# RWKV-5 scores by one product with 128 keys in place of two with 64, on one core

## The chip, the core and the metric

The kernel runs on one core of a Trainium2 chip. The metric is device time in microseconds of one execution. Three executions of the kernel before took 389.34, 387.3 and 390.62 us, median 389.34. The engines are named as in the profile: PE (TensorE; PEld are its weight loads), DVE (VectorE), ACT (ScalarE), POOL (GpSimd), SP (SyncE, which issues the loads). All data is fp32.

## What is computed

Two blocks, one after the other. The first is a linear recurrence over 768 tokens with 4 batches and 8 heads of 48 channels, the second a mixture of experts on its output:

```python
# attention: r, k, v are (4, 8, 768, 48); w, u are (8, 48)
for t in range(S):
    cur = einsum('bhd,bhe->bhde', u[None] * kt, vt)
    y[:, :, t] = einsum('bhd,bhde->bhe', rt, state + cur)
    state = w[None, :, :, None] * state + einsum('bhd,bhe->bhde', kt, vt)

# experts: x = y as (4, 768, 384), E = 8, F = 1024
e = argmax(logits[b, s]) if s == 0 or local_gate[b, s] < 0.5 else prev_e
out[b, s] = softmax(logits[b, s])[e] * (relu(x[b, s] @ w1[e]) @ w2[e])
```

## The kernel before

**Attention.** The work is cut into 16 items: 4 batches by 4 pairs of heads. The two heads of a pair lie on partitions 0 to 47 and 64 to 111. Time is cut into 6 chunks (NCH) of 128 tokens (P). Inside a chunk, the recurrence becomes a matrix of scores between 128 keys and 128 queries, masked so that a query sees only earlier keys; between chunks a state of 48 by 48 per head is carried. For each item n (functions of class `Attention`):

- `load` (L194): SP loads r and k turned (tile rk), k and v by token (kv) and v turned (vT), three items ahead.
- `scale` (L208): POOL makes ke (k times powers of w counted from the chunk's end, L217, from the table endT), rw (r times powers of w, L234; for the first three items DVE does it, in halves) and pd (r times k, L221).
- `keys` (L236): DVE makes kw, k over powers of w (L241).
- `added` (L245): PE multiplies ke by v, the sum that each chunk adds to the state (L253). `states` (L255): DVE scans these sums over the chunks into S (L259).
- `scores` (L275), called twice, for chunks 0 to 2 and 3 to 5: PE multiplies kw by rw (L288) into one of two PSUM pairs of banks, one bank per head, and DVE masks the result into tile am (L290).
- `own` (L262): PE sums u times pd over channels (L269) into tile y in PSUM, and DVE multiplies it by vT (L273).
- `inside` (L292): PE adds v times am to y (L297). `before` (L301): PE adds S times rw to y (L310), and ACT copies y to xT (L314), after which y is free for the next item's `own`.
- `turn` (L317): PE transposes xT (L323) and ACT copies it to x (L325), which goes to memory once per batch (L328). At the end of a batch, `logits` (L336) and `token_logits` (L342) make the router's inputs.

There is one y, there are two pairs of banks (shared by scores, transposes and logits, taken in turn by `banks`), two am, three rw. The order on every engine is written out by hand in `run` (L345): for an item n from 3 on it is turn(n-2), keys(n), added(n), states(n), scale(n+1), inside(n-1), before(n-1), scores(n) twice with the first mask, own(n), the second mask. From item 9 on, routing for the first two batches is put between these steps (on DVE mostly; items 13 and 14 have a step of it between the first mask and the product L273).

**The scores before.** A product of fp32 is two records of load and product in the profile. For each chunk and head, the 128 keys are taken as two halves of 64, each a product of its own (`o`). The half of later keys needs only the later 64 queries (`x`), except in the first item, where the tiles in PSUM are written in full. In odd chunks the halves change places in the 128 partitions of the result (`f`), and v (and k, in the same tile kv) is stored in that order by the host (`_tokens`). So four products lie on four quarters of the array: rows by head, columns by key half.

```python
for o in range(2):
    for h in range(2):
        q, f = slice(h * DP, h * DP + DH), c % 2 ^ o
        x = o * DP if n else 0
        nc.tensor.matmul(sc[f * DP:(f + 1) * DP, h, i, x:], lhsT=t["kw"][q, c, o * DP:(o + 1) * DP],
                         rhs=t["rw"][q, c, x:], start=True, stop=True)
```

The swap needs a second mask and a second table of end powers: `kept` (made on POOL at L1591 to L1595, doubled on ACT at L1596), and `end`, `endT` in two orders (`ends` L167 and L168, `turn_ends` L174 and L175).

**Experts.** From about 119 us on, PE multiplies blocks of tokens, gathered by expert, by w1 and w2 (L1064, L1114, L1151, L1183); POOL gathers and scatters rows. The change doesn't touch this part. `general_attention` (L477) runs only for values of w outside a range that the inputs don't have.

Of the kernel before, what the change touches and what calls it, by code (L numbers as in the profile page):

```python
# [11 lines left out]
F32 = mybir.dt.float32  # L12
# [8 lines left out]
P = 128  # L21
B, H, S, DH = 4, 8, 768, 48
HP = H // 2
# [32 lines left out]
def spread(ap, axis, n):  # L56

    a = ap.unsqueeze(axis)
    return a.to_broadcast([n if i == axis else s for i, s in enumerate(a.shape)])


class Attention:
# [10 lines left out]

    def __init__(self, tc, st, rk_d, kv_d, vT_d, x_d, w_t, wp_d, kept, ident, lt, mp):
        self.tc, self.nc = tc, tc.nc
        nc = tc.nc
        self.rk_d, self.kv_d, self.vT_d, self.x_d = rk_d, kv_d, vT_d, x_d
        self.w_t, self.kept, self.ident, self.lt = w_t, kept, ident, lt  # L80

        self.late = st.enter_context(tc.tile_pool(name="late", bufs=1))
        self.wp = self.late.tile([P, H, 32], F32, name="wp")
        self.sel = self.late.tile([P, 2 * (E + 1)], F32, name="sel")
        self.inner = ExitStack()

        def pool(name, bufs, **kw):
            return self.inner.enter_context(tc.tile_pool(name=name, bufs=bufs, **kw))

        once = pool("once", 1)  # L90
        self.two = pool("two", 2)
        self.three = pool("three", 3)
# [36 lines left out]
        n = 2  # L129
        while n <= P:  # L130
            m = min(n - 1, P + 1 - n)
            for engine, t in ((nc.vector, tab[:, :1]), (nc.gpsimd, tab[:, 1:])):
                engine.tensor_mul(t[..., n:n + m], t[..., 1:1 + m], t[..., n - 1:n].to_broadcast([P, t.shape[1], 2, m]))
            n += m

        self.first, self.newton = mp[:, :P + 1], mp[:, P + 1:2 * P + 1]
        nc.scalar.copy(self.first, tab[:, 0, 0])
        self.reciprocals(0)

        self.end = once.tile([P, HP, P + DP], F32, name="end")  # L140
        self.endT = once.tile([P, 2, HP, 2 * DH], F32, name="endT")
        self.align(26)
        self.warm(8)
        self.ends(slice(0, 1))
        self.turn_ends(slice(0, 1))
        self.warm(5)
# [17 lines left out]
            self.nc.tensor.transpose(t[:, i % 2, :P], self.ident, self.ident)  # L164

    def ends(self, z):
        self.nc.scalar.copy(self.end[:, z, :P], self.tab[:, z, 0, P - 1::-1])  # L167
        self.nc.scalar.copy(self.end[:, z, P:], self.tab[:, z, 0, P - 1:DP - 1:-1])  # L168

    def turn_ends(self, z):  # L170
        ep, n = self.banks("ep"), z.stop - z.start
        for k in range(n):
            for o in range(2):
                self.nc.tensor.transpose(ep[:, o, k * P:(k + 1) * P], self.end[:, z.start + k, o * DP:o * DP + P], self.ident)  # L174
        self.nc.scalar.copy(self.endT[:, :, z].rearrange("p o i (h d) -> p o (i h) d", h=2),  # L175
                            ep[:, :, :n * P].rearrange("p o (i d) -> p o i d", d=DP)[..., :DH])

    def tables(self):

# [28 lines left out]
    def scale(self, n):  # L208

        nc, t = self.nc, self.items[n]  # L210
        t["ke"] = self.two.tile([P, NCH, 2 * DH], F32, name="ke")
        t["pd"] = self.two.tile([P, NCH, P], F32, name="pd")
        t["rw"] = self.three.tile([P, NCH, P], F32, name="rw")
        hp = t["hp"]

        def ke(p):
            nc.gpsimd.tensor_mul(t["ke"][:, p::2], t["k"][:, p::2], spread(self.endT[:, p, hp], 1, C2))  # L217

        def pd(i):
            z = slice(i * C2, (i + 1) * C2)  # L220
            nc.gpsimd.tensor_mul(t["pd"][:, z], t["rT"][:, z], t["kT"][:, z])  # L221

        def rw(i):
            self.decayed(nc.gpsimd, n, slice(i * C2, (i + 1) * C2))


        for what in (ke, rw, pd) if n > 2 else (pd, ke):
            for i in range(2):
                what(i)
# [45 lines left out]
    def scores(self, n, g):  # L275

        nc, t = self.nc, self.items[n]
        if g == 0:
            t["am"] = self.two.tile([P, 2, 2, 3, P], F32, name="am")
        sc = self.banks("sc")[:, :, :3 * P].rearrange("p h (c t) -> p h c t", t=P)  # L280
        for i in range(3):
            c = 3 * g + i
            for o in range(2):
                for h in range(2):
                    q, f = slice(h * DP, h * DP + DH), c % 2 ^ o

                    x = o * DP if n else 0
                    nc.tensor.matmul(sc[f * DP:(f + 1) * DP, h, i, x:], lhsT=t["kw"][q, c, o * DP:(o + 1) * DP],  # L288
                                     rhs=t["rw"][q, c, x:], start=True, stop=True)
        return lambda: nc.vector.tensor_mul(t["am"][:, g], sc, spread(self.kept[:, g:g + 3], 1, 2))  # L290

    def inside(self, n):  # L292
        nc, t = self.nc, self.items[n]
# [183 lines left out]
def general_attention(tc, rk_d, kv_d, wu, wg_d, x_d, ident, lt):  # L477

    nc = tc.nc
    with tc.tile_pool(name="g1", bufs=1) as g1, tc.tile_pool(name="g2", bufs=2) as g2, \  # L480
# [3 lines left out]
        nc.vector.memset(ones, 0.0)  # L484
        for i in range(2):
            nc.vector.memset(ones[i * DP:(i + 1) * DP, i:i + 1], 1.0)
        turned = g1.tile([P, P], F32, name="g_turned")
        nc.vector.tensor_copy(turned[:, :DP], ident[:, DP:])
        nc.vector.tensor_copy(turned[:, DP:], ident[:, :DP])
        with tc.For_i(0, HP, 1) as hp:  # L490
            wu_t = g1.tile([P, 2], F32, name="g_wu")
            nc.sync.dma_start(out=wu_t, in_=wu[bass.ds(hp, 1)].rearrange("o p x -> (o p) x"))
            with tc.For_i(0, B, 1) as b:
# [11 lines left out]
                for e in range(DH):  # L505
                    vp = gps.tile([P, 2, 512], F32, name="g_vp")
                    for c in range(NCH):
                        for i in range(2):
                            nc.tensor.matmul(
                                vp[i * DP:(i + 1) * DP, c // 3, (c % 3) * P:(c % 3 + 1) * P],  # L510
                                lhsT=v_t[:, c, i, e:e + 1].to_broadcast([P, DP]),
                                rhs=turned if c % 2 else ident,
                                start=True, stop=True)
                    kv = g2.tile([P, S], F32, name="g_kv")
                    nc.vector.tensor_mul(kv.rearrange("p (g t) -> p g t", g=2),
# [1046 lines left out]
def kernel(  # L1562
# [23 lines left out]
    nc.gpsimd.affine_select(out=mask, in_=mask, compare_op=Alu.is_ge, fill=0.0, base=-1,  # L1586
                            channel_multiplier=-1, pattern=[[1, P]])

    kept = keep.tile([P, 4, P], F32, name="kept")
    lo, hi = slice(0, DP), slice(DP, P)  # L1590
    nc.gpsimd.tensor_copy(kept[:, 0], mask)  # L1591
    nc.gpsimd.memset(kept[lo, 1, lo], 0.0)
    nc.gpsimd.tensor_copy(kept[lo, 1, hi], mask[lo, lo])
    nc.gpsimd.tensor_copy(kept[hi, 1, lo], mask[hi, hi])
    nc.gpsimd.memset(kept[hi, 1, hi], 1.0)  # L1595
    nc.scalar.copy(kept[:, 2:], kept[:, :2])  # L1596
    lt = keep.tile([P, NC, E + 1], F32, name="lt")

    gid = keep.tile([P, E * ST], I32, name="gid")
# [4 lines left out]
    with ExitStack() as st, tc.manual_schedule():  # L1604
# [1 line left out]
        mpp = st.enter_context(tc.tile_pool(name="mpp", bufs=1, space=PSUM))  # L1606
        router = Router(tc, ro, mpp, lt, mask, ident, gid, sid, gate, over[:, 0:1])
        ex = Experts(tc, st, x_d, w1, w2, out, ident, router)
        att = Attention(tc, st, rk_d, kv_d, vT_d, x_d, w_t, wp_d, kept, ident, lt, router.mp)
        att.run(router, lambda: ex.fetch(0, nc.sync), lambda: ex.gather(0))  # L1610
        ex.open(st)
        router.open(1, st.enter_context(tc.tile_pool(name="ro1", bufs=1)))
# [49 lines left out]

def _tokens(a, np):

    x = a.reshape(B, HP, 2, NCH, 2, DP, DH)
    x = np.stack([x[:, :, :, c, ::-1 if c % 2 else 1] for c in range(NCH)], 2)
    return x.transpose(0, 1, 4, 5, 2, 3, 6).reshape(B, HP, P, NCH * 2 * DH)


# [35 lines left out]
```

## Time and profile before

| what | us |
|---|---|
| median of three runs | 389.34 |
| profiled execution, its own time | 388.15 |
| its span in the profile | 386.4 |
| attention: first score product to last product L310 | 7.4 to 115.8 |
| first expert product L1064 | 119.5 |
| L288, scores on PE, busy | 22.4 |
| L290, masking on DVE, busy | 30.1 |
| L269, busy | 14.1 |
| L297, busy | 28.9 |

A line of the profile gives the program's line, the engine, the operation, its tiles as out<-in, shapes as partitions by elements, and a count. In timelines the columns are start and length in us of a run of like instructions, and in brackets the engine's idle time before it with what ended it. "issue" there is idle time in which no semaphore was awaited. Matmul records overlap: their lengths include the passage through the array, so the time from first start to last end is what counts.

### The profile page before, as it was taken

How to read it: one execution, taken by the hardware profiler on the slowest of the kernel's cores; microseconds unless marked ns; L12 is line 12 of the kernel's file. 1: busy time of each engine (PE TensorE's matmuls, PEld its weight loads, DVE VectorE, ACT ScalarE, POOL GpSimd, SP SyncE). 2: the span in 40 equal slices, each digit the busy share in tenths (PEclk: the TensorE clock that was granted, in tenths of full speed). 3: DMA queues.
4: the chain of work that ended last, by engine and by line, in shares of the span. 5: the costliest groups of instructions: out<-in, count | busy, mean ns of one | idle time of the engine just before them, and what ended most of it. 6: DMA issues, size and time to landing. Idle time of an engine off the chain costs nothing. (4 is left out here: it accounts for less than half of the span.)

```text
span 386.4 us, 9723 instructions
## 1 busy us (share of the span) xinstructions
PE 371.5 (96%) x3858; PEld 328.5 (85%) x3858; DVE 247.1 (64%) x718; ACT 107.6 (28%) x293; POOL 151.1 (39%) x212
## 2 busy tenths in 40 slices
PE   7999999799999999999999999999999999999992
PEld 6776877677777999998999999999999999999971
DVE  7887576588954564587657757758757758556400
ACT  4132232222213111322323233234224234222220
POOL 8769998696322022611333222312403213012022
PEclk9999999999999999999999999999999999999998
DMA  7999998979213982740552145245156146064011
GB/s 257 414 409 410 409 405 274 355 256 394 99 32 101 378 338 64 249 185 23 184 179 108 42 170 213 66 171 204 56 185 224 38 165 227 21 199 181 2 37 37
DMA packets 17477, 74.97 MB, mean 194 GB/s; under 512 B 2729, under 2 KB 6586, under 8 KB 14864
## 3 DMA queue, kind: packets, MB, share of 16 engines
q1 hardware_dynamic: 10048, 56.89, 39.1%
q0 software_dynamic: 3424, 9.52, 7.4%
q10 hardware_dynamic: 3952, 7.87, 5.6%
q8 instruction: 32, 0.52, 0.6%
q14 instruction: 21, 0.17, 0.1%
HBM read 64.83 MB, written 9.51 MB: 192 GB/s over the span
## 5 line engine op out<-in xcount | busy, mean ns | idle before, releaser
L1263 POOL DMA_INDIRECT out_dram<-yo,sid x27 | 26.6, 986 | 102.3 <-ACT yo L1258 78.8
L1114 PE MATMUL h<-exT,w1t 128*128 128x168 f32 (+4 forms) x240 | 54.9, 327 | 0.0
L1118 DVE TENSOR_TENSOR hT<-h,hs 128x168 f32<-128x168 f32 (+3 forms) x60 | 21.1, 351 | 46.5 <-PE h L1114 30.4
L1037 POOL DMA_INDIRECT xg<-x_d,gid x29 | 31.1, 1073 | 38.2 <-DVE sm L872 17.4
L1114 PEld LDWEIGHTS h<-exT,w1t 128*128 128x128 f32 x240 | 41.7, 190 | 0.3 <-issue 0.3
L290 DVE TENSOR_TENSOR am<-pair,kept 128x768 f32<-128x768 f32 x32 | 30.1, 952 | 16.8 <-PE pair L288 16.4
L1064 PE MATMUL h<-exT,w1t 128*128 128x192 f32 (+1 forms) x192 | 38.2, 337 | 0.0
L1183 PE MATMUL y<-factors,sums 128*128 128x192 f32 x168 | 36.8, 326 | 0.0
L1114 PE MATMUL h<-xs,ws 128*128 128x168 f32 (+4 forms) x144 | 35.2, 326 | 0.0
L1064 PEld LDWEIGHTS h<-exT,w1t 128*128 128x128 f32 x192 | 32.3, 190 | 1.4 <-issue 0.2
L221 POOL TENSOR_TENSOR pd<-rk 128x384 f32<-128x384 f32 x32 | 31.9, 1017 | 3.0 <-DMA rk<-in_rk_dram 2.2
L297 PE MATMUL y<-am,kv 128*64 128x128 f32 x384 | 28.9, 278 | 3.4 <-issue 2.2
L1114 PEld LDWEIGHTS h<-xs,ws 128*128 128x128 f32 x144 | 25.5, 190 | 4.3 <-ACT hs L1121 1.2
L1183 PEld LDWEIGHTS y<-factors,sums 128*128 128x128 f32 x168 | 28.9, 190 | 0.0
L297 PEld LDWEIGHTS y<-am,kv 128*64 128x64 f32 x384 | 24.8, 136 | 4.7 <-issue 2.4
L234 POOL TENSOR_TENSOR rw<-rk,tab 128x384 f32<-128x384 f32 x26 | 23.6, 931 | 7.3 <-PE y L310 7.3
L217 POOL TENSOR_TENSOR ke<-kv,endT 128x288 f32<-128x288 f32 x32 | 24.9, 799 | 3.9 <-DMA kv<-in_kv_dram 3.0
L314 ACT COPY xT<-y 128x768 f32<-128x768 f32 (+1 forms) x16 | 12.5, 779 | 42.3 <-PE y L310 42.3
L288 PE MATMUL pair<-rw,kw 48*64 48x128 f32 (+1 forms) x768 | 22.4, 249 | 1.3 <-ACT end L168 0.6
L1183 PE MATMUL y<-w2t,hT 128*128 128x192 f32 x96 | 23.0, 328 | 0.0
L1051 DVE COPY exT<-tp 128x384 f32<-128x384 f32 (+6 forms) x29 | 14.0, 489 | 12.8 <-PE tp L1050 12.6
L288 PEld LDWEIGHTS pair<-rw,kw 48*64 48x64 f32 x768 | 19.4, 133 | 2.7 <-issue 0.9
(279 smaller groups left out, 733.0 us busy)
## 6 DMA issues: line engine op xcount, KB each, us to landing
w1t<-in_w_dram SPq DMA_DIRECT2D x9, 1536.0 KB, 6.7
w2t<-in_w_dram SPq DMA_DIRECT2D x9, 1536.0 KB, 7.3
rk<-in_rk_dram SPq DMA_DIRECT2D x15, 768.0 KB, 9.4
kv<-in_kv_dram SPq DMA_DIRECT2D x16, 584.0 KB, 9.1
vT<-in_vT_dram SPq DMA_DIRECT2D x16, 384.0 KB, 7.4
x_d<-x ACTq DMA_DIRECT2D x4, 1152.0 KB, 10.7
w1t<-in_w_dram ACTq DMA_DIRECT2D x1, 1536.0 KB, 10.2
w2t<-in_w_dram ACTq DMA_DIRECT2D x1, 1536.0 KB, 13.5
```

What stands on the lines that cost most here:

```text
L217: nc.gpsimd.tensor_mul(t["ke"][:, p::2], t["k"][:, p::2], spread(self.endT[:, p, hp], 1, C2))
L221: nc.gpsimd.tensor_mul(t["pd"][:, z], t["rT"][:, z], t["kT"][:, z])
L234: engine.tensor_mul(t["rw"][:, z], t["rT"][:, z], spread(pw, 1, z.stop - z.start))
L288: nc.tensor.matmul(sc[f * DP:(f + 1) * DP, h, i, x:], lhsT=t["kw"][q, c, o * DP:(o + 1) * DP], rhs=t["rw"][q, c, x:], start=True, stop=True)
L290: return lambda: nc.vector.tensor_mul(t["am"][:, g], sc, spread(self.kept[:, g:g + 3], 1, 2))
L297: nc.tensor.matmul(t["y"][p * DP:(p + 1) * DP, h, c2 * P:(c2 + 1) * P], lhsT=t["v"][:, (2 * c + h) * DH:(2 * c + h) * DH + DP], rhs=t["am" ...
L1037: self.nc.gpsimd.indirect_dma_start(out=xg[:n], out_offset=None, in_=self.x_d[:rows], in_offset=bass.IndirectOffsetOnAxis(ap=u["gid"][:n, ...
L1064: nc.tensor.matmul(h[:, :n], lhsT=u["w1"][:, m, kk, :], rhs=u["xT"][:, kk, :], start=(kk == 0), stop=(kk == DK - 1))
L1114: nc.tensor.matmul(out, lhsT=a, rhs=b, start=start and k == 0, stop=stop and k == len(terms) - 1, skip_group_check=True)
L1118: nc.vector.tensor_tensor(out, a, b, op=Alu.add)
L1183: return lambda: nc.tensor.matmul(bank[:, x * half:(x + 1) * half], lhsT=a, rhs=b, start=(j == 0 and x == 0), stop=(j == FK // 2 - 1), ski ...
L1263: self.nc.gpsimd.indirect_dma_start(out=out.rearrange("n (h d) -> (n h) d", h=2) if half else out, out_offset=bass.IndirectOffsetOnAxis(ap ...
```

## The change

For each chunk and head there is one product: 128 keys, 128 queries, with the result on all 128 partitions. Keys are in the same order in every chunk, so one mask serves all chunks, read three times over by DVE, and one table of end powers. ke is made for chunks 0 to 2 and then 3 to 5, in place of even and then odd ones. The host stores k and v in plain order.

```diff
-        self.end = once.tile([P, HP, P + DP], F32, name="end")
-        self.endT = once.tile([P, 2, HP, 2 * DH], F32, name="endT")
+        self.end = once.tile([P, HP, P], F32, name="end")
+        self.endT = once.tile([P, HP, 2 * DH], F32, name="endT")
...
     def ends(self, z):
-        self.nc.scalar.copy(self.end[:, z, :P], self.tab[:, z, 0, P - 1::-1])
-        self.nc.scalar.copy(self.end[:, z, P:], self.tab[:, z, 0, P - 1:DP - 1:-1])
+        self.nc.scalar.copy(self.end[:, z], self.tab[:, z, 0, P - 1::-1])
...
         for k in range(n):
-            for o in range(2):
-                self.nc.tensor.transpose(ep[:, o, k * P:(k + 1) * P], self.end[:, z.start + k, o * DP:o * DP + P], self.ident)
+            self.nc.tensor.transpose(ep[:, 0, k * P:(k + 1) * P], self.end[:, z.start + k], self.ident)
...
-        def ke(p):
-            nc.gpsimd.tensor_mul(t["ke"][:, p::2], t["k"][:, p::2], spread(self.endT[:, p, hp], 1, C2))
+        def ke(i):
+            z = slice(i * C2, (i + 1) * C2)
+            nc.gpsimd.tensor_mul(t["ke"][:, z], t["k"][:, z], spread(self.endT[:, hp], 1, C2))
...
             c = 3 * g + i
-            for o in range(2):
-                for h in range(2):
-                    q, f = slice(h * DP, h * DP + DH), c % 2 ^ o
-
-                    x = o * DP if n else 0
-                    nc.tensor.matmul(sc[f * DP:(f + 1) * DP, h, i, x:], lhsT=t["kw"][q, c, o * DP:(o + 1) * DP],
-                                     rhs=t["rw"][q, c, x:], start=True, stop=True)
-        return lambda: nc.vector.tensor_mul(t["am"][:, g], sc, spread(self.kept[:, g:g + 3], 1, 2))
+            for h in range(2):
+                q = slice(h * DP, h * DP + DH)
+                nc.tensor.matmul(sc[:, h, i], lhsT=t["kw"][q, c], rhs=t["rw"][q, c], start=True, stop=True)
+        return lambda: nc.vector.tensor_mul(t["am"][:, g], sc, spread(spread(self.mask, 1, 3), 1, 2))
...
-    kept = keep.tile([P, 4, P], F32, name="kept")
-    lo, hi = slice(0, DP), slice(DP, P)
-    nc.gpsimd.tensor_copy(kept[:, 0], mask)
-    nc.gpsimd.memset(kept[lo, 1, lo], 0.0)
-    nc.gpsimd.tensor_copy(kept[lo, 1, hi], mask[lo, lo])
-    nc.gpsimd.tensor_copy(kept[hi, 1, lo], mask[hi, hi])
-    nc.gpsimd.memset(kept[hi, 1, hi], 1.0)
-    nc.scalar.copy(kept[:, 2:], kept[:, :2])
...
-    x = a.reshape(B, HP, 2, NCH, 2, DP, DH)
-    x = np.stack([x[:, :, :, c, ::-1 if c % 2 else 1] for c in range(NCH)], 2)
-    return x.transpose(0, 1, 4, 5, 2, 3, 6).reshape(B, HP, P, NCH * 2 * DH)
+    return a.reshape(B, HP, 2, NCH, P, DH).transpose(0, 1, 4, 3, 2, 5).reshape(B, HP, P, NCH * 2 * DH)
```

`general_attention` loses the turned identity that undid the swap.

More of the change, by code (lines that the diff above doesn't have):

```diff
@@ L62, with __init__ @@
 class Attention:
-    def __init__(self, tc, st, rk_d, kv_d, vT_d, x_d, w_t, wp_d, kept, ident, lt, mp):
+    def __init__(self, tc, st, rk_d, kv_d, vT_d, x_d, w_t, wp_d, mask, ident, lt, mp):
         self.tc, self.nc = tc, tc.nc
@@ L79, in __init__ @@
         self.rk_d, self.kv_d, self.vT_d, self.x_d = rk_d, kv_d, vT_d, x_d
-        self.w_t, self.kept, self.ident, self.lt = w_t, kept, ident, lt
+        self.w_t, self.mask, self.ident, self.lt = w_t, mask, ident, lt
         self.late = st.enter_context(tc.tile_pool(name="late", bufs=1))
@@ L172, in turn_ends @@
         for k in range(n):
-            for o in range(2):
-                self.nc.tensor.transpose(ep[:, o, k * P:(k + 1) * P], self.end[:, z.start + k, o * DP:o * DP + P], self.ident)
-        self.nc.scalar.copy(self.endT[:, :, z].rearrange("p o i (h d) -> p o (i h) d", h=2),
-                            ep[:, :, :n * P].rearrange("p o (i d) -> p o i d", d=DP)[..., :DH])
+            self.nc.tensor.transpose(ep[:, 0, k * P:(k + 1) * P], self.end[:, z.start + k], self.ident)
+        self.nc.scalar.copy(self.endT[:, z].rearrange("p i (h d) -> p (i h) d", h=2),
+                            ep[:, 0, :n * P].rearrange("p (i d) -> p i d", d=DP)[..., :DH])
     def tables(self):
@@ L486, in general_attention @@
             nc.vector.memset(ones[i * DP:(i + 1) * DP, i:i + 1], 1.0)
-        turned = g1.tile([P, P], F32, name="g_turned")
-        nc.vector.tensor_copy(turned[:, :DP], ident[:, DP:])
-        nc.vector.tensor_copy(turned[:, DP:], ident[:, :DP])
         with tc.For_i(0, HP, 1) as hp:
@@ L511, in general_attention @@
                                 lhsT=v_t[:, c, i, e:e + 1].to_broadcast([P, DP]),
-                                rhs=turned if c % 2 else ident,
+                                rhs=ident,
                                 start=True, stop=True)
@@ L1608 @@
         ex = Experts(tc, st, x_d, w1, w2, out, ident, router)
-        att = Attention(tc, st, rk_d, kv_d, vT_d, x_d, w_t, wp_d, kept, ident, lt, router.mp)
+        att = Attention(tc, st, rk_d, kv_d, vT_d, x_d, w_t, wp_d, mask, ident, lt, router.mp)
         att.run(router, lambda: ex.fetch(0, nc.sync), lambda: ex.gather(0))
```

## The prediction

> **What bounds the kernel now.** I read the page first, then busy time by stage, then the sum of waits, then the timeline of single items. A change of 1% (3.9 us) is about what a measurement of this kernel can tell from no change. The page:
>
> ```profile
> span 386.4 us, 9723 instructions
> PE 371.5 (96%) x3858; PEld 328.5 (85%) x3858; DVE 247.1 (64%) x718; ACT 107.6 (28%) x293; POOL 151.1 (39%) x212
> ...
> POOL out_dram L1263 0%
> ...
> L288 PE MATMUL pair<-rw,kw 48*64 48x128 f32 (+1 forms) x768 | 22.4, 249 | 1.3 <-ACT end L168 0.6
> ```
>
> The chain that ended last is of no use here: it stops at the final scatter (0% of the span). PE is busy 96%, but the scores (L288) hold only 22.4 us of it, all in attention. So the stage decides:
>
> ```profile
> core 0: us, PE busy (x) PEld busy (x) DVE busy (x) ACT busy (x) POOL busy (x), PEclk, DMA share, GB/s
> 10.00:60.00 50.00, 47.97 (x1006) 37.88 (x1007) 37.40 (x73) 12.79 (x32) 44.80 (x61) 1.00 1.01 404
> 60.00:119.00 59.00, 55.73 (x1095) 41.51 (x1088) 42.48 (x74) 15.00 (x33) 34.15 (x38) 1.00 0.62 221
> ```
>
> From 10 to 60 us the DMA share is full and POOL is at 44.80 of 50, which looks like two other bounds. The waits say no: in all of attention POOL waited for rk and kv only 5.2 us, in the first four items, and its longest recurring wait (L234, 7.3 us) is for a buffer that PE frees. Loads and POOL run ahead and are held back by PE. What sets an item's period is read in one undisturbed item (number 7):
>
> ```profile
> 52.14 0.49 PE L297 MATMUL y<-am,kv 128*64 128x128 f32 x3
> ...
> 52.56 1.30 PE L310 MATMUL y<-rw,S 48*48 48x128 f32 x20
> ...
> 53.68 1.19 PE L288 MATMUL pair<-rw,kw 48*64 48x128 f32 x48
> 53.92 0.80 ACT L314 COPY xT<-y 128x768 f32<-128x768 f32 x1 [2.91 <-PE y L310]
> 54.48 0.96 DVE L290 TENSOR_TENSOR am<-pair,kept 128x768 f32<-128x768 f32 x1 [1.57 <-PE pair L288]
> ...
> 54.87 0.88 PE L269 MATMUL y<-pd,w_t 48*64 48x384 f32 x8
> 55.67 0.58 PEld L323 LDWEIGHTS pair<-ident,xT 112*128 112x128 f32 x6 [0.60 <-DVE am L290]
> ...
> 55.86 0.97 DVE L273 TENSOR_TENSOR y<-y,vT 128x768 f32<-128x768 f32 x1 [0.42 <-PE y L269]
> ...
> 56.88 1.94 PE L297 MATMUL y<-am,kv 128*64 128x128 f32 x24
> ```
>
> A ring: the state product L310 ends at 53.86; ACT copies y out (ends 54.72) while PE does the scores (53.68 to 54.87); then L269 may overwrite y (54.87), DVE multiplies it (55.86 to 56.83), L297 starts at 56.88, then L310 of the next item. So L269 starts 1.01 us after L310's end, gated by the copy, with the scores ending just as it starts. The scores have almost no cover to grow into. Two more rows price the change:
>
> ```profile
> 11.50 1.55 PE L297 MATMUL y<-am,kv 128*64 128x128 f32 x24
> ```
>
> ```profile
> PEld y L310 <- issue: 3.1, 16, 0.4
> ...
> PEld y L297 <- issue: 2.4, 1, 2.4
> ```
>
> **The change part by part.**
>
> *Scores.* Per chunk and head, before: two products of 64 keys, one with 128 and (from item 1 on) one with 64 moving columns; a product is two records. An item has 48 records, on four quarters of the array (head by key half), and takes 1.19 us from first start to last end. After: 24 records, all with 128 moving columns, on two halves (head only, each 48 rows by 128 columns). The nearest row is L297 at 11.50: also 24 records of 128 moving columns on two halves of the array, nothing awaited: 1.55 us. So fewer instructions take 0.36 us longer: the masked quarter that was skipped is now computed, and in each of the two halves 12 records follow each other at about 0.11 us.
>
> *Two changes of shape.* Before, L310, L288 and L269 all ran on quarters, and L288 started 0.18 us ahead of L310's end (53.68 against 53.86). Where the shape changes, from L297 to L310, the next product started only 0.07 us ahead of the end (52.56 against 52.63); that is the 0.17 to 0.19 us of idle per item in the wait of L310 for "issue" (3.1 over 16). After, this change comes twice more, before and after the scores. New ring: scores start 0.07 before L310's end, last 1.55, L269 starts 0.07 before their end: 1.55 - 0.14 = 1.41 us after L310's end against 1.01 now. Delay per item +0.40 us. L269 to L323 (0.08 ahead) and L323 to L253 (0.06) agree. Low end, no price for the change of shape: 1.55 - 0.36 = 1.19, +0.18 us. High end, no overlap, the next shape starting only at the end of the old: 1.55, +0.54 us.
>
> *A rule on the drain.* In the rows above the next shape starts 0.06 to 0.08 us ahead of the old one's modelled end. The Trainium skill, TensorEngine Tiling (Array Packing), Key Properties, says that changing the tiling mode, not just the tile, drains the engine; that speaks against this change, and an estimate by it, with no overlap left, is +6.8 us in all. By the rows it is the +5.0 below.
>
> *Weight loads.* The new loads are 128 columns wide; in the trace L342, with 128 columns and 18 moving, does 6 records in 0.84 us with matmuls of 0.27, so 0.11 us a load. Two such streams in parallel fit the 0.11 us spacing of the products. If the two row halves had to share one load path, 24 loads would take 23 x 0.114 + 0.27 = 2.9 us and the delay would be 1.75 us (high end). Against this: 48 loads of 133 ns now finish within 1.14 us with both heads' quarters of one column half going at once. I take parallel.
>
> *A rule on loads.* In the expert stage six records of L1151 (192 moving columns) took 1.14 us with matmuls of 0.33, a spacing of 0.16, with a 190 ns load for each: the loads are hidden in the same rows. The Trainium skill, TensorE: Matmul & The Clock Gate, Part 3, says that a load overlaps running products only where the row group differs; with its load time of columns over 1.2 per ns, an estimate by it is 12 x (0.107 + 0.109) = 2.6 us for the scores. The row decides.
>
> *Who takes the delay on.* L269 late makes DVE's L273 late, then L297, then L310 of the next item: one to one. Behind L269 on PE are also the transposes L323 (now waiting 0.60 for L290) and L253; they move with it, and the wait on L290 vanishes behind the later L269. DVE's first L290 starts later by 0.28 us (half of the scores: 0.80 now, about 0.97 then, plus the 0.11 later start); L273 comes later still, so it doesn't count, except in items 13 and 14, where routing work sits between L290 and L273 on DVE and the 0.28 passes instead of the 0.40. SP's loads and POOL's steps wait for buffers freed by this ring and shift with it; both have lead.
>
> *Items 0 to 2* make kw and rw in halves on DVE and the second half of the scores waits for it; only half the excess shows: 0.2 each in items 1 and 2. Item 0 already computed all 128 columns (half of its scores then lie under the wait): 0.
>
> *Masks.* L290 reads one mask three times instead of three tables. L241 reads its operand repeated over chunks and takes 945 ns for 128x768; L290 takes 952. Nothing, bounds ±0.01 us a call.
>
> *ke.* POOL's L217 takes three neighbouring chunks in place of every second; same 128x288, 799 ns. L253's first products need one half instead of both. POOL has lead: nothing, and if L217 cost 0.1 more, the 5.1 to 5.6 us of POOL's steps stay under the 6.2 us period.
>
> *Start.* Five POOL instructions on the mask table (1.71 to 2.86 us) go, but POOL's next step waits for DVE's w at 3.17, so nothing; if that cover went, 1.2 us at most. ACT loses L1596 (0.40) and L168, off the path: L288 first waits for DVE's rw. PE loses three of six transposes L174 between items 0 and 1 (0.87 us for six, 0.116 each): L253 could start 0.35 earlier, its ke being ready at 10.26, and the scan behind it too: -0.35.
>
> *Instruction supply.* PE loses 388 pairs of load and product. It once waited 2.4 us for "issue" (L297 at 74.0) with no semaphore in the way; the page has a DMA queue of instructions. Fewer instructions may remove that wait (-2.4) or move it: I take 0.
>
> **Sum.** Items 3 to 12: 10 x 0.40 = 4.0. Items 13, 14: 0.56. Item 15: 0.40. Items 1, 2: 0.40. Start: -0.35. Together +5.0 us. The expert stage (119 us on) is unchanged, begins with PE right behind the last item, and shifts. The profiled execution took 388.15 us (span 386.4), so 393.2; the median of the three runs (389.34) is 1.2 above it and would give 394.3. I predict 393.8.
>
> **Rivals.**
> 1. *The shape change is free, or the long wait for instructions goes.* For it: all changes of shape that the trace shows change the number of rows too (128 to 48 and back); here the two heads' rows stay and only the columns change. With +0.18: 1.8 + 0.2 + 0.18 + 0.2 - 0.35 = +2.0, so 390 to 391.5; with the 2.4 gone as well, no change, 388 to 389. Against it: L310's idle for "issue" is there in all 16 items.
> 2. *The weight loads of the two heads don't run in parallel.* +1.75 in 11 items, about half of it in four more, so some +22 us: 410 or more. Against it: the four quarters of now.
> 3. *Not slower.* Place: L269, which now waits for ACT's copy and not for the scores. If the 24 records end within 1.0 us of L310's end, the ring keeps its period; that needs 1.1 us in place of 1.55, so records on the two halves spaced below 0.08. Then the gains alone count, -0.35 and perhaps -2.4: 385.5 to 389. Against it: L297's spacing.
>
> **How the numbers follow.** My forecast (0.40, up to 0.54 an item) 0.65; rival 1 0.18; rival 2 0.10; rival 3 0.07. The forecast's own range is 391.6 to 396.2: half way between rival 1 and the sum (+3.5) on the profiled 388.15, and +6.8 (0.54 an item, in the order of the sum: 5.4 + 0.7 + 0.54 + 0.54 - 0.35 = 6.8) on the median 389.34. The range of 8 in 10 reaches down into rival 1 (389.5) and up to 398 (+6.8 on the highest run shown, 390.62, rounded up); left out are rival 2 and the lowest cases. Slower by over 1% needs +3.9: three quarters or more of the forecast, all of rival 2 and little of rival 1: 0.63. Within 1%: the rest of the forecast, rival 1 and most of rival 3: 0.33. Faster by over 1%: 0.04.
>
> **What the profile after would show.** Scores: 24 records in about 1.55 us, starting 0.07 ahead of L310's end, with "issue" idle before them and before L269; L269 about 1.4 us after L310's end, no longer just behind the copy; L297 starting later by the same; L290 still 0.95 us; L323 no longer waiting for L290; the end of the last L310 near 120.8 instead of 115.8. I'm wrong if scores take 1.2 us (rival 3), 2.9 us (rival 2), if L288 starts 0.18 ahead as before (rival 1), or if the items' period stays near 6.2 us although the scores are longer, which would mean that another ring sets it.

## The result, and the profile after

Twelve runs of each kernel, side by side: before 388.29 us (387.30 to 390.79), after 391.24 us (391.09 to 391.63). The ratio is 1.0066, 95% interval 1.0047 to 1.0086: slower, by 2.95 us and not by the 5 of the prediction. The profiled executions took 388.15 and 391.09, spans 386.4 and 389.4, so the two traces hold the whole difference. Lines of the changed kernel stand 1 to 8 lower than before: L284 are the scores (L288 before), L285 the masks, L268 the product into y (L269), L272 the product with vT (L273), L292 (L297), L305 the state product (L310).

From the page of the changed kernel:

```profile
span 389.4 us, 8940 instructions
PE 377.1 (97%) x3470; PEld 333.2 (86%) x3470; DVE 246.3 (63%) x718; ACT 106.5 (27%) x290; POOL 149.8 (38%) x207
...
q8 instruction: 29, 0.48, 0.5%
...
L285 DVE TENSOR_TENSOR am<-pair,mask 128x768 f32<-128x768 f32 x32 | 30.1, 952 | 17.5 <-PE pair L284 17.5
...
L284 PE MATMUL pair<-rw,kw 48*128 48x128 f32 x384 | 26.3, 282 | 0.8 <-DVE rw L233 0.7
```

PE has 388 loads and 388 products less, and is busy 5.6 us longer. The masks cost 952 ns as before. The busy time of the scores rises only from 22.4 to 26.3; what counts is their place in the ring. Busy time by stage (the second stage ends 2 us later than the one shown of before):

```profile
core 0: us, PE busy (x) PEld busy (x) DVE busy (x) ACT busy (x) POOL busy (x), PEclk, DMA share, GB/s
10.00:60.00 50.00, 48.90 (x803) 38.69 (x802) 36.32 (x72) 12.54 (x32) 44.72 (x60) 1.00 1.01 398
60.00:121.00 61.00, 60.14 (x929) 45.38 (x926) 42.68 (x75) 14.99 (x33) 34.60 (x39) 1.00 0.63 221
```

PE's idle time in the first stage falls from 2.03 to 1.10 us, in the second from 3.27 of 59 to 0.86 of 61: PE waits less than before, and its chain is longer. Item 7 in the timeline:

```profile
54.45 0.90 PE L305 MATMUL y<-rw,S 48*48 48x128 f32 x20
...
55.29 1.61 PE L284 MATMUL pair<-rw,kw 48*128 48x128 f32 x24
55.40 0.80 ACT L309 COPY xT<-y 128x768 f32<-128x768 f32 x1 [2.50 <-PE y L305]
56.27 0.96 DVE L285 TENSOR_TENSOR am<-pair,mask 128x768 f32<-128x768 f32 x1 [1.47 <-PE pair L284]
...
56.83 0.88 PE L268 MATMUL y<-pd,w_t 48*64 48x384 f32 x8
57.63 0.58 PEld L318 LDWEIGHTS pair<-ident,xT 112*128 112x128 f32 x6 [0.60 <-DVE am L285]
...
57.83 0.97 DVE L272 TENSOR_TENSOR y<-y,vT 128x768 f32<-128x768 f32 x1 [0.59 <-PE y L268]
```

The state product ends at 55.35. The scores start 0.06 before that, take 1.61, and L268 starts 0.07 before their end, 1.48 after the state product's end (1.01 before); ACT's copy had ended at 56.20. An undisturbed item takes 6.26 us; before, the least disturbed took 5.78. So the bare price is 0.48 us an item. (Item 7 of before, shown ahead of the result, isn't undisturbed: its L310 holds a wait, as follows.)

**Where the rest went.** The end of the state product of each item, after minus before, in us (worked out from the two traces):

| item | 0 | 1 | 2 | 3 | 4 | 5 | 6 | 7 | 8 | 9 | 10 | 11 | 12 | 13 | 14 | 15 |
|---|---|---|---|---|---|---|---|---|---|---|---|---|---|---|---|---|
| shift | 0.0 | 0.34 | 0.68 | 1.16 | 1.08 | 1.42 | 1.50 | 1.57 | 1.90 | -0.25 | 0.11 | 0.59 | 1.07 | 1.29 | 1.70 | 2.23 |

Items 3, 11 and 12 show the full 0.48. In items 4 to 9 the kernel before loses time of its own, most of it in item 9. There its PE waits without a semaphore. The weight loads of the kernel before at these places, in its timeline ("issue" is the wait):

```profile
34.04 0.75 PEld L288 LDWEIGHTS pair<-rw,kw 48*64 48x64 f32 x33 [0.60 <-issue]
...
53.16 0.48 PEld L310 LDWEIGHTS y<-rw,S 48*48 48x48 f32 x16 [0.36 <-issue]
...
59.35 0.48 PEld L310 LDWEIGHTS y<-rw,S 48*48 48x48 f32 x16 [0.36 <-issue]
...
74.04 0.68 PEld L297 LDWEIGHTS y<-am,kv 128*64 128x64 f32 x12 [2.40 <-issue]
```

Together 3.7 us. Counted along all records of PE in order of time (loads, products and its sequencer's, four an item), these waits stand at numbers 1218, 1986, 2242 and 2754, all 194 more than a multiple of 256. Call these places borders, and what lies between two a block. The page's queue q8 of instructions has 32 packets in 0.52 MB before and 29 after: 16 KB each, which is 64 bytes for each of 256 records. From 25 to 82 us, before, such a packet starts 3.3 to 6.0 us after the last border and takes 1.0 to 1.1 us, and in eight of nine blocks PE passes the next border 1.3 to 1.4 us after the packet's end: PE waits for its instructions, a little or much. After, the packets start nearly as late (2.1 to 4.1 us, one early), but a block lasts 7.3 to 8.6 us (before 5.9 to 6.9 with the waits, one 8.3), and the next has landed 3.3 to 6.4 us ahead. In the wait sums of the changed kernel only the usual gap before the state product is left:

```profile
PEld y L305 <- issue: 2.4, 14, 0.2
```

The last 0.8 us of the difference arise in the expert stage. In the timeline of the changed kernel ACT takes over h 2.1 us after the product L1056 that made it:

```profile
146.57 1.24 PE L1056 MATMUL h<-exT,w1t 128*128 128x192 f32 x6
...
148.62 1.14 PE L1056 MATMUL h<-exT,w1t 128*128 128x192 f32 x6
149.89 0.55 ACT L1059 ACTIVATE hT<-h 128x192 f32<-128x192 f32 x2 [4.59 <-PE h L1056]
150.28 1.24 PE L1143 MATMUL y<-hT,w2t 128*128 128x192 f32 x6 [0.52 <-ACT hT L1059]
```

The first of these products ends at 147.81; its signal to ACT is recorded at 149.81, with that of the next one. PE's weight loads then stand idle for 0.81 us. Before, ACT had taken each over within 0.1 us. That this belongs to the change isn't shown: from the last state product to the end, the kernel before and six of the others below take 270.6 us, the changed one and seven others 271.3 to 271.5, and both groups hold kernels of either shape of the scores (the two with a general path, below, left out).

### The profile page after: what moved, and what is told of

It reads as the page before. It is cut to its first block, busy times and chain, and to the rows that moved or that the text cites. A ratio compares the mean times of both kernels' runs of the same rounds, so it can differ in the third digit from the quotient of the medians.

```text
span 389.4 us, 8940 instructions
## 1 busy us (share of the span) xinstructions
PE 377.1 (97%) x3470; PEld 333.2 (86%) x3470; DVE 246.3 (63%) x718; ACT 106.5 (27%) x290; POOL 149.8 (38%) x207
## 5 line engine op out<-in xcount | busy, mean ns | idle before, releaser
L285 DVE TENSOR_TENSOR am<-pair,mask 128x768 f32<-128x768 f32 x32 | 30.1, 952 | 17.5 <-PE pair L284 17.5
L1056 PE MATMUL h<-exT,w1t 128*128 128x192 f32 (+1 forms) x192 | 38.2, 337 | 0.0
L1056 PEld LDWEIGHTS h<-exT,w1t 128*128 128x128 f32 x192 | 32.3, 190 | 1.4 <-issue 0.2
L292 PE MATMUL y<-am,kv 128*64 128x128 f32 x384 | 28.2, 278 | 1.1 <-DVE y L272 1.0
L284 PE MATMUL pair<-rw,kw 48*128 48x128 f32 x384 | 26.3, 282 | 0.8 <-DVE rw L233 0.7
L292 PEld LDWEIGHTS y<-am,kv 128*64 128x64 f32 x384 | 24.3, 136 | 2.1 <-DVE y L272 1.5
L284 PEld LDWEIGHTS pair<-rw,kw 48*128 48x128 f32 x384 | 23.0, 187 | 3.5 <-ACT end L167 0.9
```

Of the source, the lines that this page charges most:

```text
L284: nc.tensor.matmul(sc[:, h, i], lhsT=t["kw"][q, c], rhs=t["rw"][q, c], start=True, stop=True)
L292: nc.tensor.matmul(t["y"][p * DP:(p + 1) * DP, h, c2 * P:(c2 + 1) * P], lhsT=t["v"][:, (2 * c + h) * DH:(2 * c + h) * DH + DP], rhs=t["am" ...
L1056: nc.tensor.matmul(h[:, :n], lhsT=u["w1"][:, m, kk, :], rhs=u["xT"][:, kk, :], start=(kk == 0), stop=(kk == DK - 1))
```

## The experiments

The theory: *PE's instructions arrive in blocks of 256 and come late while the loads fill the DMA engines; the kernel before uses a block up too fast and waits, the changed one doesn't.* Rivals: the waits belong to the order or shape of PE's instructions; or the difference is the price of an item alone, and the waits are an accident of one profile.

**Lighter loads, in both kernels.** From item 4 on, rk and vT without the unused partitions, as two loads of 48:

```diff
+        if n >= AHEAD:
+            for h in range(2):
+                q = slice(h * DP, h * DP + DH)
+                nc.sync.dma_start(out=rk[q].rearrange("p a c t -> p (a c t)"), in_=self.rk_d[b, hp][q])
...
-        nc.sync.dma_start(out=vT.rearrange("p a c t -> p (a c t)"), in_=self.vT_d[b, hp])
+        for q in [slice(h * DP, h * DP + DH) for h in range(2)] if n >= AHEAD else [slice(0, P)]:
+            nc.sync.dma_start(out=vT[q].rearrange("p a c t -> p (a c t)"), in_=self.vT_d[b, hp][q])
```

The kernel before so changed:

> The kernel before, with the loads of rk and vT from item 4 on cut to the 96 partitions that hold data (1448 in place of 1736 KB an item); the zero rows stay from the first loads, the result is the same. Theory A (supply): in the kernel before, PE waited at multiples of 256 of its own instructions (2.40, 0.60, 0.36 and 0.36 us in the profile), because a block of instructions comes by DMA and is late while the loads fill the DMA engines; the changed kernel needs a block every 7.8 us in place of 6.2 and lost these waits, some 3.7 us, against some +6 from a longer ring. With 17% less to load the blocks come earlier: 385 to 387 us against 388.3, and the long waits at blocks gone or shorter. Theory B (no supply): these waits have another cause and the ring is only longer by half of what I took: within 0.5 us of the kernel before.

The changed kernel so changed:

> The changed kernel with the same lighter loads. Theory A: it has no wait for instructions to lose, so 391.2 +-0.7 us. Theory B: the same. If it gains as much as the kernel before does from lighter loads, both theories are wrong about where the loads count.

Measured: 402.57 us, ratio 1.0406 (1.0386 to 1.0427), and 397.94, ratio 1.0305 (1.0264 to 1.0346), both against the kernel before at 386.79. It decides nothing between the theories, since loads with fewer bytes were the slower ones, and POOL now waited for kv (3.0 us before):

```profile
L222 POOL TENSOR_TENSOR ke<-kv,endT 128x288 f32<-128x288 f32 x32 | 24.9, 798 | 28.9 <-DMA kv<-in_kv_dram 24.8
```

The busy shares from 30 to 70 us, first of the kernel with the 48-partition loads, then of the kernel before:

```profile
30.00:70.00 40.00, 35.84 (x729) 26.76 (x728) 25.16 (x48) 10.29 (x27) 28.82 (x42) 1.00 0.94 225
```

```profile
30.00:70.00 40.00, 39.19 (x800) 30.11 (x799) 27.29 (x57) 10.97 (x28) 38.35 (x54) 1.00 0.96 368
```

The engines are as full as before (0.94, 0.96) at 225 GB/s in place of 368; in this stretch the median packet of 6 KB took 446 ns in place of 235, and one of kv, whose loads are as before, 295 in place of 180. One thing follows nevertheless: in the changed kernel packets of instructions now started up to 6.8 us after the last border and took 1.1 to 1.5, and waits at borders appeared there too, 1.63 us at 42.9 and 0.84 at 76.0. In these two blocks the packet's start, its time and the 1.9 and 1.7 us until PE went on add up to 10.0 and 8.6 us, where the same blocks last 8.5 and 7.7 in the changed kernel as it is. Its scores don't protect it.

**The scores taken apart.** Two parts of the change alone: the changed kernel with two 64-key products again (plain order, one mask, one table of end powers), and the kernel before with all 128 queries computed in both halves.

```diff
+                for o in range(2):
+                    x = o * DP if n else 0
+                    nc.tensor.matmul(sc[o * DP:(o + 1) * DP, h, i, x:], lhsT=t["kw"][q, c, o * DP:(o + 1) * DP],
+                                     rhs=t["rw"][q, c, x:], start=True, stop=True)
```

```diff
-                    x = o * DP if n else 0
+                    x = 0
```

> The changed kernel (keys in plain order, one mask, one table) with the two products of 64 keys put back, so quarters of the array without the swap. The half with early keys is always on the same two quarters: 12 records of 0.109 us in a row there, so the scores take about 1.3 us from first start to last start in place of 0.95, with no change of shape on either side: L269's line starts 1.40 us after the last start of the state product, against 1.26 before and 1.73 in the changed kernel. As many PE instructions as before. Ring alone: +0.14 x 13 = +1.8 us on the kernel before. Theory A (late instructions set the pace of items 3 to 11 in the kernel before): there the longer ring uses up time that PE lost anyway, +0.3 to +1.2 us. So 387 to 388.6 where the kernel before takes 386.8, well below the changed kernel.

> The kernel before with all 128 queries in both key halves: on quarters, with the swap, the masked quarter computed, no change of shape, the same count of instructions. Each quarter does 12 records of 0.109 us, as in the run without the swap: the same +0.14 us of ring an item, so the same time as that run within 0.5 us. If computing the masked quarter were all of the change's cost, this would come near the changed kernel (+4 us).

Measured: 388.13, ratio 1.0015 (0.9995 to 1.0036), and 387.72, ratio 1.0005 (0.9980 to 1.0030), beside 387.23. Both profiles keep the waits at borders (0.31 to 1.91 us in five; 0.34, 0.61 and 2.60). The plain order, the mask and the table cost nothing that can be told. The masked quarter hardly does either. In the timeline of the second kernel:

```profile
53.07 0.93 PE L310 MATMUL y<-rw,S 48*48 48x128 f32 x20
53.81 1.49 PE L288 MATMUL pair<-rw,kw 48*64 48x128 f32 x48
54.06 0.80 ACT L314 COPY xT<-y 128x768 f32<-128x768 f32 x1 [2.53 <-PE y L310]
55.12 0.83 PE L269 MATMUL y<-pd,w_t 48*64 48x384 f32 x8
```

The scores take 1.49 us in place of 1.19, but start 0.19 ahead of the state product's end and overlap L269 by 0.18, so that L269 starts 1.12 after that end: 0.11 more than before, and its undisturbed items take 5.85 to 5.90. Of the 0.48 us an item some 0.1 is the masked quarter; the other 0.37 is the shape on two halves, with its small overlaps of 0.06 and 0.07.

**Later loads and stores.** In the kernel before: loads two items ahead in place of three; or the first three stores of x on SP's queue in place of ACT's.

```diff
-AHEAD = 4
+AHEAD = 3
```

```diff
-            nc.scalar.dma_start(out=self.x_d[b * S:(b + 1) * S, :].rearrange("(c p) d -> p c d", p=P), in_=x)
+            (nc.scalar if n > B * HP - 3 else nc.sync).dma_start(out=self.x_d[b * S:(b + 1) * S, :].rearrange("(c p) d -> p c d", p=P), in_=x)
```

> The kernel before with loads two items ahead in place of three. Theory A: less is asked for at the start, the DMA engines are full for a shorter time (to some 45 us in place of 60), PE's instructions come in time earlier: 1 to 2 us faster, fewer waits at multiples of 256 after 45 us. If no wait at these places changes, the loads are not what makes the instructions late. If the loads then come too late for POOL, it gets slower, with DMA waits of L217 or L221.

> The kernel before with the stores of x of the first three batches (1152 KB each) issued by SP behind the loads in place of ACT beside them. The 2.40 us wait at a multiple of 256 stood while such a store was under way. Theory A with the store as part of the crowd: that wait gets shorter, 1 to 2 us faster. If only the loads matter: within 0.5 us.

Measured: 390.06, ratio 1.0104 (1.0042 to 1.0165), and 386.59, ratio 0.9976 (0.9954 to 0.9997), beside 387.23. In the profile of the first (388.00 us, its lowest time), items 3 and 5 to 7 take 5.77 to 5.78, no wait at a border is left, and PE is 3.4 us ahead at item 9. That is given back in item 13 (9.46 us in place of 6.29). There the later loads lie beside the fetch of the experts' weights: from 90 to 110 us the DMA share was 0.65 (0.46 before), and the granted clock 0.91 (1.00); which of the two it was isn't shown. The second kept its waits (0.31, 0.37, 0.63, 1.84 us); it is the fastest kernel of this study, by a quarter of a per cent (the interval ends just below 1).

**Paced loads.** Two items ahead through item 9, then three, in the kernel before, the changed one, and the plain one with 64-key products and the stores on SP; and beside them a test of ACT's late h, three unread copies on ACT in the changed kernel that restore the number of its instructions.

```diff
+RK = (1, 3, 0, 1, 3, 0, 1, 3, 0, 1, 2, 3, 0, 1, 2, 3)
+KV = (3, 4, 1, 2, 3, 4, 1, 2, 3, 4, 0, 1, 2, 3, 4, 0)
...
-            if n + AHEAD - 1 < M:
-                self.load(n + AHEAD - 1)
+            for i in range(n + AHEAD - 2 if n < 10 else n + AHEAD - 1, min(n + AHEAD - 1 if n < 9 else n + AHEAD, M)):
+                self.load(i)
```

```diff
+        self.nc.scalar.copy(self.spare[:, z], self.tab[:, z, 0, P - 1:DP - 1:-1])
...
+    nc.scalar.copy(keep.tile([P, 2, P], F32, name="unread"), spread(mask, 1, 2))
```

> The kernel before, with loads two items ahead through item 9 (three rk and vT buffers and four kv buffers in use) and three ahead after that; items 11 and 12 are loaded in one go to catch up. Nothing else differs. Theory (PE's instructions come late while loads fill the DMA engines): the four waits without a semaphore in the items up to 9 (3.7 us) go or fall under 1 us in all, undisturbed items are 5.78 us apart, and the last state product ends at 112 to 113.5 in place of 115.8. The time is 384 to 386 if nothing later takes it back, and about 387 if the double load brings one late block back. Rival (the waits belong to the order of instructions on PE, whatever the loads do): four waits as before, the end at 115.8, 387 to 388. Second rival (with fewer buffers POOL or DVE wait for data): waits with a semaphore for rk or kv on POOL of 1 us or more per item, and no gain.

> The changed kernel with the same loads as in the run before it in this list. Theory: it has no late instructions to lose, so nothing is gained: undisturbed items 6.26 us apart, the last state product ends at 118.0 (+-0.3), 390.7 to 391.7. Against the paced kernel before, this is the cost of the two products' new shape without the instruction waits: 0.48 us for each of the items 3 to 15 and 0.35 for items 1 and 2, 5.5 to 7 us at the last state product. Rival (loads slow the ring itself, in both kernels alike): this one gains as much as the kernel before does, and the difference stays near 2.2 us at the last state product.

> A try for a faster version: the changed kernel's plain key order, one mask and one end table, but the scores by two products of 64 keys as before; the paced loads of the first run in this list; and the first three stores of x issued on SP's queue in place of ACT's. Theory: as the paced kernel before, and 0 to 1 us less for the stores: 383.5 to 386. Rival (the plain order costs something that the loads hid): above the paced kernel before by 0.5 us or more.

> The changed kernel plus three copies on ACT that nothing reads (two of the second end table's size, one of the second half of the masks), so that ACT has as many instructions ahead of the expert stage as before. Theory (ACT's late hT at 149.9 us, 0.8 us of idle PE after it, comes from where ACT's instruction blocks now end): the idle 0.8 us goes, the shift against before in the expert stage is the 2.2 us of attention, 390.2 to 390.7. Rival (the transfer or the semaphore that ACT waited for is late by itself): the 0.8 us stays, 391.0 to 391.6.

Measured, beside 388.32: 389.57, ratio 1.0029 (0.9998 to 1.0060); 391.37, 1.0079 (1.0048 to 1.0109); 390.78, 1.0054 (1.0025 to 1.0083); 391.27, 1.0080 (1.0053 to 1.0108).

Pacing did not remove the waits, against the theory: the first has six, of 0.33 to 1.18 us, 4.0 in all, and packets that start 3.1 to 4.5 us after a border. The ring sets how many bytes are loaded in an item, and the DMA share from 50 to 70 us was 0.99 (0.90 before), so the engines were no emptier. So the profile of the loads two items ahead, with packets that start after 0.7 to 3.1 us from 28 to 78 us, isn't explained by its buffers, which the paced kernel shares up to item 9. Nor do full engines alone make a packet late: from 20 to 60 us the DMA share of that profile was 0.98. What makes a packet start early or late stays open, and with it the theory's part on the loads. In the changed kernel pacing did nothing, as expected: the same periods of 6.26 and no wait.

The copies on ACT did nothing: h is late as it was (0.79 us of idle PE). It is late in both paced kernels with 64-key products too (0.79 at 148.3, 0.78 at 148.9), and not in the changed kernel with the 48-partition loads. So it comes neither from ACT's number of instructions nor from the shape of the scores; its cause stays open. The version that was to be faster has waits of 1.32, 0.53, 1.08 and 1.45 us, and two under 0.3.

**More instructions at the same work.** Small products of four moving columns, ahead of L269 from item 3 on, into columns of y that nothing reads: 12 in the kernel before, 12 and 24 in the changed one.

```diff
+        for i in range(12 if n > 2 else 0):
+            p, h = divmod(i % 4, 2)
+            q, x = slice(h * DP, h * DP + DH), C2 * P + 4 * (i // 4)
+            nc.tensor.matmul(y[p * DP:(p + 1) * DP, h, x:x + 4], lhsT=self.w_t[q, t["hp"], 1:2].to_broadcast([DH, DP]),
+                             rhs=t["pd"][q, 0, :4], start=True, stop=True)
```

An earlier pair of runs had 12 of them behind L269, where they disturb what y accumulates, so that a general path ran behind attention (2782.13 and 2778.67 us in all) and only the attention stage can be read:

> The kernel before with 12 small products more per item from item 3 on, behind the product of u (quarters of the array, 4 moving columns, into columns of y that nobody reads): 48 instructions of PE more per item, 300 in place of 252. By themselves they cost PE some 0.35 us an item (24 records on four quarters at about 0.014 us), 13 items: +4.5 us. Theory A: in items 3 to 11 PE gets 256 instructions per 6.2 us, so 300 take 7.3 us an item in place of 6.1: +8 to +11 us, with waits at multiples of 256. Theory B: +4.5 us, no more waits than before.

> The changed kernel with the same 12 small products per item: 252 instructions per item, as many as the kernel before. Theory A: an item then takes 6.3 + 0.35 us and the supply gives 252 in 6.1, so no wait: +4.5 us on the changed kernel, up to +6 if the supply is a little slower. Theory B: +4.5 us, the same amount as in the kernel before.

The last state product ended at 125.60 (115.80 + 9.8), with nine waits at borders, 8.7 us in all, and at 121.68 (118.03 + 3.65), with none. Then, ahead of L269:

> The kernel before, with 12 products of 4 moving columns put ahead of each item's L269 from item 3 on, into columns of y that nothing reads: 48 more records of load and product an item, 300 in place of 252. Theory (a block of 256 PE instructions takes about 6.1 us to come while the loads run, so a ring that uses one up sooner waits): unstalled, an item would take about 6.15 us and a block 5.2, so PE waits at most block borders up to 85 us, 6 to 10 us in all; the last state product ends near 125 and the time is 396 to 399. Rival (instruction supply plays no part; the added products only take their own 0.3 to 0.4 us an item): 388 + 13 x 0.37 = 393, with no more waits than before.

> The changed kernel with the same 12 products: 252 records an item, as many as the kernel before has. Theory: an item takes 6.26 + 0.3 = 6.56 us, so a block takes 6.66, still longer than the 6.1 it needs to come: no wait, last state product near 121.7, 394.5 to 395.5, and so faster than the kernel before with the same 12 products, though without them it is slower. Rival (what decides is the number of records an item, not the time in which a block is used up): waits like those of the kernel before, 3 us or more in all, 397.5 or more.

> The changed kernel with 24 such products: 300 records an item. Theory: unstalled 6.26 + 0.6 = 6.86 us an item and 5.85 us a block, under 6.1: the waits without a semaphore appear, at numbers 256 apart, 0.2 to 1 us each and 1 to 5 us in all; 399.5 to 403. Rival (the changed kernel's scores are free of such waits for another reason): none, last state product near 125.3, 398.2 to 399.2.

Measured, beside 390.11: 406.0, ratio 1.0397 (1.0324 to 1.0469); 397.88, ratio 1.0195 (1.0148 to 1.0242); 402.78, ratio 1.0329 (1.0276 to 1.0381). With the same 48 records more in each, the changed kernel is the faster one by 8 us. What a block lasts when nothing is awaited (256 over the records of an item, the sequencer's four included, times its period) sorts them:

| kernel | records an item | period, us | block, us | waits at borders, 25 to 85 us |
|---|---|---|---|---|
| before | 256 | 5.78 | 5.78 | 4 |
| before + 12 | 304 | 6.12 | 5.15 | 7 |
| after | 208 | 6.26 | 7.70 | 0 |
| after + 12 | 256 | 6.61 | 6.61 | 0 |
| after + 24 | 304 | 6.96 | 5.86 | 2 |

The waits come back in the changed kernel. In the timeline of its 24 products:

```profile
36.87 0.59 PEld L268 LDWEIGHTS y<-pd,w_t 48*64 48x64 f32 x33
38.01 0.26 PEld L268 LDWEIGHTS y<-pd,w_t 48*64 48x64 f32 x12 [0.55 <-issue]
```

and in its wait sums:

```profile
PEld y L297 <- issue: 1.4, 1, 1.4
```

They stand at numbers 1218 and 1986, as before's do. And the kernel before with 12 has the larger ones, here from its timeline:

```profile
68.86 0.44 PEld L253 LDWEIGHTS mp<-kv,ke 128*48 128x48 f32 x16
70.45 0.17 PEld L253 LDWEIGHTS mp<-kv,ke 128*48 128x48 f32 x4 [1.15 <-issue]
```

So it is the time in which a block is used up, and not the shape of the scores or the number of records of an item: 256 records wait at 5.78 us a block and not at 6.61. The whole times of the first two came out above what was expected, that of the changed kernel with 12 (397.88) in its rival's range; but the rival's waits are not in its profile (of its fastest execution, 396.57). The kernel before, run beside them, was itself 1.8 us above the median of the first comparison; in the last item the added products move DVE's product with vT behind the transposes (1.1 us in the changed kernel with 12); and the kernel before with 12, after waits of 6.5 us up to 85 us, waited again from 102 and 109 us (1.93, 1.31), where none was expected, and had a granted clock of 0.92 and 0.91 from 60 to 100 us.

## Why the prediction was right or wrong

- **The ring** (state product, copy and scores, L269, L273, L297) was right, and so was the sign. L269's start moved from the copy's end to the scores' end, as said.
- **Scores**: 1.55 forecast, 1.61 measured, 0.06 above the row taken; the records follow each other at 0.11 us on each half, as said, but for the first two (0.21).
- **The item that was read** (number 7 of before) was called undisturbed and wasn't: its L310 took 1.30 us, with the wait of 0.36 at 53.16 in it, where it takes 0.90 in the changed kernel. So a period of 6.2 us, named as the ring's, has such a wait in it; without it, it is 5.78. Nothing in the sum rests on it.
- **Changes of shape**: starts 0.07 ahead forecast, 0.06 and 0.07 measured. The Trainium skill, TensorEngine Tiling (Array Packing), Key Properties, says that a change of tiling mode drains the engine; the trace shows a start-up that overlaps by only 0.06 us where the same shape overlapped by 0.18, which is nearer to the page than to no price, and the run with all queries puts 0.37 us an item on the shape.
- **Delay per item**: 0.40 forecast, 0.48 measured; over items 3 to 12 4.8 in place of 4.0. Items 13 and 14: 0.63 in place of 0.56. Item 15: 0.53 in place of 0.40. Items 1 and 2: 0.34 each in place of 0.20.
- **Start**: -0.35 forecast, nothing measured (item 0's state product ends at the same time). The transposes start 0.20 us later, behind longer scores of item 0, which were put at 0, and L252 then waits 0.17 for POOL's ke, itself 0.50 later than before behind a load of kv.
- **Masks, ke, row halves in parallel**: right (952 ns and 797 ns, spacing 0.11). Twenty-four loads of 187 ns fit into 1.42 us: they run beside products on their own rows. The Trainium skill's rule, TensorE: Matmul & The Clock Gate, Part 3, by which 2.6 us were estimated, doesn't hold here (1.61 measured). That L323 would no longer wait for L290 was wrong (0.60 as before) and cost nothing.
- **Instruction supply: the step that failed**, a term put at 0 without a count. "Fewer instructions may remove that wait (-2.4) or move it: I take 0." It removed that one, three more and the small ones around them. The bare prices add up to 4.8 + 0.63 + 0.53 + 0.68 = 6.6 us; 2.2 was left at the end of attention, so 4.4 came back, 3.7 of it in the four waits listed. The row was seen and named; what was not done was to look at the other waits of that kind and at where they stand in PE's sequence. Two of them were inside a row that was shown: L310's 3.1 us for "issue" in 16 items are the two waits of 0.36 and 14 gaps of 0.17, not a gap in every item; after, it is 2.4 in 14.
- **Expert stage**: "unchanged, and shifts" was wrong by the 0.8 us of the late signal, with its cause open. 2.2 + 0.8 = 3.0, the difference of the spans.

## What to carry to other kernels

When a wait has no semaphore, count where it stands along the engine's instructions: waits at equal distances point to late instructions, which added small products can test, and then a change in the number of instructions has a price or a gain of its own, to be put into the sum. Work out how long a block lasts at the ring's period and compare it with the time its packet takes from the last border. And a change of array shape inside a ring costs on both sides even when it halves the instructions; the masked work that it adds can be the smaller part.

## What was not expected of the hardware

- From 25 to 82 us, with the DMA engines 0.95 busy, PE's blocks of 256 instructions took about 6 us from border to use in the kernel before (3.3 to 6 to start, 1.0 to move, 1.3 until PE goes on), so that some 42 records a microsecond were a bound of their own. With loads two items ahead it was less, for a reason that stays open.
- Loads to 48 partitions, with fewer bytes, took longer for each packet (446 ns for 6 KB against 235), and so did the whole loads of kv beside them (295 against 180); they held the DMA engines as full at 225 GB/s as whole ones did at 368.
- The twelve times of the kernel before lie 3.5 us apart, those of the changed one 0.5. That fits waits that vary from run to run and are gone after the change; no experiment was made on it.
- A product's signal can come 2.0 us late with no work to show for it, in the changed kernel and in seven others, of either shape of the scores.
